# A planner's order for four token blocks: traced durations, layer chains first and steps placed by readiness from the second block on, and a last block without GpSimd

## The chip, the cores and the metric

One core of a Trainium2 chip (trn2) runs the whole program. The metric is the device time of one execution in microseconds (us); several executions of a kernel are timed and their median is compared.

## What is computed

The reference is a causal attention followed by two feed-forward layers, cut here to what matters:

```python
# q, k, v: 4 x 8 heads x 576 x 64;  s: 4 x 8 x 576
scores = q @ k.T / sqrt(64)
cum    = cumsum(max(s, 0))
scores = where(causal, -1e9, scores + min(-(cum_i - cum_j), 0))
attn   = softmax(scores)                    # rows of 576
x      = (attn @ v)                         # 2304 tokens x 512
# layer 1, d_ff 1536
x = ((x @ w_a) * (x @ w_b)) @ w_out
# layer 2, d_ff 2048
h = x @ w_in
g = max(h, 0) + alpha * min(h, 0)
out = g @ w_out
```

All in float32. The kernel keeps that accuracy by cutting each float32 operand into a high and a low part and doing three matmuls for one.

## The kernel before

**Tiling.** The 2304 tokens go through the layers in four blocks of 512, 512, 512 and 768 (`blk` 0 to 3). `ffn` computes one block: layer 1 is a loop over 12 tiles of d_ff (`NF1`), each with two matmul groups in (`into`) and one out, layer 2 a loop over 16 (`NF2`). `mm3` (L1231 to L1233) issues the three matmuls: high by high (`xh`, `wh`), low by high (`xl`), high by low (`wl`); the outs of layer 2 are L1824 to L1826. The last block (`SEVEN` = 3) goes through `ffn_seven` instead, which replaces eight products of half tiles by seven; its tiles `mt`, `th`, `tl` are sums of halves of x, `sw`, `wm`, `wa` sums of weights, `d` partial products.

**What stands between the matmuls.** An intermediate tile is cut on ScalarE (high part: L281) and VectorE or GpSimd (low part: `sub`, L295). The same is done for each weight tile (`wh`, `wl` from `raw`). Weights of the first block, and a third of the second block's, arrive as 64-bit values (`raw<-in_w_dram`) and are decoded by ScalarE (`top`, L1012) and VectorE, and the decoded ones are kept in DRAM (`w_d`) for later blocks.

**Attention as steps.** The attention of the next block is cut into steps (`s01`, `s23`, `s4` for scores and softmax, matmuls at L520; `two_av` for the product with v, matmuls at L845 and L784), and the steps are put between the matmuls of the current block's feed-forward layers. `z` are scores, `zt` their transposes on the way through DRAM (`zd`), `cb` the bias loaded from `cum_d`, `mn` and `sm` the row statistics.

**What sets the order.** Every engine runs its instructions in the order in which they were recorded. The recorder, `Order`, holds a model of the engines' times: `run.now` is TensorE's time in the model, moved on by `run.pe` for each group of matmuls. Work of the other engines is written as chains (`spawn`); `_first` picks the chain whose next instruction can start first by the model, a tie goes to the smaller `time + slack`; `need` runs chains until a given one is done, `pump` runs what can start before `run.now`. `Either` lets the recorder pick GpSimd or VectorE by their modelled time. Three numbers set the model's cost: `gap` (ns added per matmul), `act` and `dve` (ns per instruction on ScalarE and VectorE): `AS_PLANNED` for blocks 0 to 2, `AS_TRACED` for block 3. Steps are put in at a steady rate:

```python
want = min(len(steps), (i + 1) * len(steps) * FASTER / total)
while done < want:
    f, args = steps[done]
    f(*args)
    done += 1
```

where i counts the pieces of the feed-forward layers issued so far.

Of the kernel before, what the change touches and what calls it, by code (L numbers as in the profile page):

```python
# [9 lines left out]
F32 = mybir.dt.float32  # L10
# [5 lines left out]
AF = mybir.ActivationFunctionType  # L16
# [49 lines left out]
FROM_WEIGHTS, AHEAD, FROM_LEAD, FROM_STEPS, STEPS = 2, 10, 3, 4, 3  # L66


FASTER, BEFORE = 1.06, 6


SEVEN, PLAIN_1, PLAIN_2 = 3, 3, 4
SL_SEVEN, SL_BANK = 2500.0, -2000.0
AS_PLANNED, AS_TRACED = (0.0, 90.0, 70.0), (13.3, 170.0, 155.0)
A11, A12, S1, S3, S2, S4, A22 = range(7)


# [29 lines left out]
class Order:  # L107
# [7 lines left out]
    def __init__(self):  # L115
        self.now, self.t, self.n = 0.0, 0.0, 0
        self.free, self.open, self.late = {}, [], LATE
        self.use(AS_PLANNED)

    def use(self, times):  # L120
        self.gap, self.act, self.dve = times

    def spawn(self, gen, ready=None, slack=0.0):
        c = Chain(gen)
# [84 lines left out]
def attention_two_moe_kernel(  # L209
# [77 lines left out]
    def dve(n, rate, f, *args, port=False, **k):  # L287
        yield {"dve2" if port else "dve": run.dve + rate * n}, SEEN
        f(*args, **k)  # L289

    def sub(o, i0, i1, sbuf=True):
        n = size(o)
        t = run.dve + 1.04 * n
        eng = yield Either(pool=115 + 2.17 * n, dve2=t) if sbuf else {"dve": t}, SEEN
        (nc.gpsimd if eng == "pool" else nc.vector).tensor_tensor(o, i0, i1, op=ALU.subtract)  # L295

    def tt(o, i0, i1, op):
        n = size(o)
        eng = yield Either(pool=115 + 2.17 * n, dve2=run.dve + 1.04 * n), SEEN
        (nc.gpsimd if eng == "pool" else nc.vector).tensor_tensor(o, i0, i1, op=op)  # L300

    def scale(o, i, s0, s1):
        n = size(o)
        eng = yield Either(pool=115 + 1.09 * n, dve2=run.dve + 0.52 * n), SEEN
# [21 lines left out]

    ident = const.tile([P, P], F32, name="ident")
    make_identity(nc, ident)
    alpha_sb = small.tile([P, NF2], F32, name="alpha_sb", bufs=1)

    banks = [ps.tile([P, 512], F32, name=f"bank{i}") for i in range(8)]
# [889 lines left out]
    def take():  # L1221
        nonlocal taken
        taken += 1
        prefetch()
        got, ready = loaded[taken - 1]
        run.need(ready)
        return got


# [4 lines left out]
        run.pe(3 * (o.shape[-1] / 2.4 + run.gap))  # L1234

    o_done = {}

    t_hl, pools = [], {}
    H2 = blocks[-1][1] // 2
# [2 lines left out]
    def open_seven():  # L1242

        inner.close()
        big = ctx.enter_context(tc.tile_pool(name="big", bufs=1))

        def big_tile(shape, dtype, tag, bufs=1):
            return big.tile(shape, dtype, name=tag, tag=tag, bufs=bufs)

        pools["big"] = big_tile  # L1250
        t_hl[:] = [
            [big_tile([P, 2, H2], F32R, f"t{j}{i}") for j in "hl"] for i in range(4)
        ]
# [128 lines left out]
    def ffn_seven(blk, sums):  # L1382
# [83 lines left out]

        def rectified_parts(f, got, g, m):
            yield from act(m, g, AF.Relu, scale=-1.0)
            yield from scale(m, m, alpha_sb[:, f:f + 1], -1.0)
            yield from dve(  # L1470
                T, 1.04, nc.vector.scalar_tensor_tensor, g, g, 0.0, m, op0=ALU.max,
                op1=ALU.add, port=True,
            )
            yield from split_g(got, g)
            run.give(of_d, run.t)
# [244 lines left out]
    def ffn(blk):  # L1720
# [5 lines left out]
        def into(j):  # L1726
            wh, wl = take()
            if j in used:
                run.need(used[j])
# [14 lines left out]
        def split_g(f, g):  # L1744
            gh = gp.tile([P, T], F32R, name="gh", tag="gh")
            gl = gp.tile([P, T], F32R, name="gl", tag="gl")
            g_done[f] = gh, gl, run.spawn(split_t(g, gh, gl), run.t)

        def copy_a():
            yield of_t  # L1750
# [37 lines left out]
        for f in range(NF1 + 1):  # L1788
            if f < NF1:
                yield from into(0)  # L1790
                used[0] = run.spawn(copy_a())
                yield from into(1)
                run.need(used[0])
                used[1] = run.spawn(gate(f))
            if f >= 1:
                wh, wl = take()
                gh, gl, ready = g_done.pop(f - 1)
                run.need(ready)
                for d in range(KD):
                    c = slice(d * P, (d + 1) * P)  # L1800
                    o = acc[d][:, 0:T]
                    if f == 1 and d in o_done:
                        run.need(o_done[d])
                    mm3(o, wh[:, c], wl[:, c], gh, gl, f == 1, f == NF1)
                    if f == NF1:
                        x2[d] = run.spawn(
                            split_by(o, xhb[:, d, 0:T], xlb[:, d, 0:T], SHRUNK ** 2)
                        )
                    if d == KD - 1:
                        run.give(of_w)  # L1810
                    yield

        for f in range(NF2 + 2):
            if f < NF2:
                yield from into(f % 2)
                used[f % 2] = run.spawn(rectify(f, ab[f % 2][:, 0:T]))
            if f >= 2:
                wh, wl = take()
                gh, gl, ready = g_done.pop(f - 2)
                run.need(ready)  # L1820
# [23 lines left out]
    for blk in range(NB):  # L1844
        scarce = blk == 0
        run.late = LATE_0 if scarce else LATE
        run.use(AS_TRACED if blk == SEVEN else AS_PLANNED)
        T = blocks[blk][1]
        while x_done[blk]:
            run.need(x_done[blk].pop(0))  # L1850
        steps = plan[blk][1]
        if blk + 1 < NB:
            steps[-BEFORE:-BEFORE] = plan[blk + 1][0]
        if 1 <= blk < NB - 1:
            n = max(0, blk * S + QA - blocks[blk + 1][0])
# [3 lines left out]
        done = 0  # L1859
        if blk == SEVEN:  # L1860
            open_seven()
        for i, _ in enumerate(ffn_seven(blk, sum_x()) if blk == SEVEN else ffn(blk)):
            want = min(len(steps), (i + 1) * len(steps) * FASTER / total)
            while done < want:
                f, args = steps[done]
                f(*args)
                done += 1
        assert done == len(steps)
    while run.open:
        run._run(run._first())  # L1870

# [58 lines left out]
```

## Time and profile before

| | |
|---|---|
| median of 3 executions | 998.69 us (998.48 to 1001.89) |
| the profiled execution: its time, its span in the profile | 998.6 us, 996.6 us |
| PE (TensorE matmuls) busy | 969.5 us, 97% of the span |
| DVE (VectorE) busy | 755.4 us, 76% |
| ACT (ScalarE) busy | 543.4 us, 55% |
| POOL (GpSimd) busy | 310.3 us, 31% |
| first FFN matmuls of blocks 1, 2, 3 | 276.6, 496.7, 717.0 us |

The span is the part of an execution that the profiler shows; 2.0 us lie outside it. Busy time is a sum over the instructions of an engine, so an engine at 97% has 27 us without work in the whole span, and it is there that an order can win or lose time. Times below are from the start of the span.

### The profile page before, as it was taken

To read this page: it belongs to the slowest core of one execution; us is meant where nothing else is said; L and a number is where in the kernel's file an instruction comes from. 1 tells how busy PE (TensorE), PEld (TensorE's weight loads), DVE (VectorE), ACT (ScalarE), POOL (GpSimd) and SP (SyncE) were. 2 spreads that over 40 slices of the span, in tenths; PEclk is the share of its full clock that TensorE was granted. 3 is DMA by queue.
4 is the path that set the end of the run, shared out by engine and by line. 5 is a ranking of instruction groups with operands and counts; after the bars stand their busy time and mean duration, and the time that the engine had idled before them with its cause. 6 is when DMAs were issued, how large, how long until landed. Compare 5 with 4: busy or idle time off the path is not lost.

```text
span 996.6 us, 16041 instructions
## 1 busy us (share of the span) xinstructions
PE 969.5 (97%) x5291; PEld 811.7 (81%) x5291; DVE 755.4 (76%) x1689; ACT 543.4 (55%) x1144; POOL 310.3 (31%) x361
## 2 busy tenths in 40 slices
PE   6999999999999989999999999999999999999998
PEld 4567777778888867888888888888889999988886
DVE  7787777886769667887579877676596888697782
ACT  5966665776656455754555555544452333554342
POOL 2131121431225323442134334231233334252320
PEclk9999999999999999999999999999999999999999
DMA  7699999899688879778498787647312213021101
GB/s 192 189 287 325 340 304 325 300 332 316 233 286 249 270 220 297 227 228 255 142 273 268 220 251 238 207 138 204 141 41 87 65 64 102 26 75 53 63 1 63
DMA packets 140082, 196.77 MB, mean 197 GB/s; under 512 B 35744, under 2 KB 79776, under 8 KB 140000
## 3 DMA queue, kind: packets, MB, share of 16 engines
q1 hardware_dynamic: 130208, 177.93, 57.0%
q10 hardware_dynamic: 9792, 17.83, 4.8%
q8 instruction: 41, 0.67, 0.3%
q14 instruction: 41, 0.34, 0.1%
HBM read 152.13 MB, written 43.59 MB: 196 GB/s over the span
## 4 chain that ended last, share of the span: by engine, by line
PE 85%; DVE 6%; DMA 4%; issue 2%; ACT 2%; SPq 0%; POOL 0%; ACTq 0%; POOLq 0%; DVEq 0%
PE bank L1231 19%; PE bank L1232 18%; PE bank L1233 18%; PE bank L1824 5%; PE bank L1826 4%; PE bank L1825 4%; PE bank L784 3%; DMA raw<-in_w_dram 2%; PE bank L1674 2%; PE bank L1672 2%; PE bank L1673 2%; PE bank L520 2%; PE bank L724 1%; PE bank L546 1%; PE bank L845 1%
## 5 line engine op out<-in xcount | busy, mean ns | idle before, releaser
L1231 PE MATMUL bank<-xh,wh 128*128 128x512 f32 (+1 forms) x620 | 239.9, 387 | 4.5 <-DVE d L289 2.0
L1232 PE MATMUL bank<-xl,wh 128*128 128x512 f32 (+1 forms) x620 | 234.9, 379 | 2.0 <-DVE xl L289 2.0
L1233 PE MATMUL bank<-xh,wl 128*128 128x512 f32 (+1 forms) x620 | 234.6, 378 | 0.0
L281 ACT ACTIVATE wh<-raw 128x512 fp32r<-128x512 f32 (+1 forms) x197 | 114.5, 591 | 84.1 <-PE bank L1232 28.4
L295 POOL TENSOR_TENSOR wl<-raw,wh 128x512 fp32r<-128x512 f32 (+1 forms) x74 | 98.7, 1337 | 161.9 <-ACT wh L281 129.9
L1231 PEld LDWEIGHTS bank<-xh,wh 128*128 128x128 f32 x620 | 116.9, 189 | 30.9 <-issue 5.7
L1232 PEld LDWEIGHTS bank<-xl,wh 128*128 128x128 f32 x620 | 117.0, 189 | 21.8 <-DVE xl L289 3.1
L1233 PEld LDWEIGHTS bank<-xh,wl 128*128 128x128 f32 x620 | 116.7, 188 | 19.0
L273 ACT ACTIVATE z<-z,mn 128x128 f32<-128x128 f32 (+4 forms) x144 | 82.8, 577 | 54.6 <-DVE mn L289 52.8
L295 DVE TENSOR_TENSOR wl<-raw,wh 128x512 fp32r<-128x512 f32 (+1 forms) x130 | 89.4, 694 | 29.4 <-ACT wh L281 26.0
L1231 PE MATMUL bank<-gh,wh 128*128 128x512 f32 (+1 forms) x240 | 89.1, 371 | 0.0
L1233 PE MATMUL bank<-gh,wl 128*128 128x512 f32 (+1 forms) x240 | 88.8, 370 | 0.0
L1232 PE MATMUL bank<-gl,wh 128*128 128x512 f32 (+1 forms) x240 | 88.7, 369 | 0.1
L1012 ACT ACTIVATE top<-raw 128x512 f16<-128x512 bf16 x90 | 69.3, 784 | 27.4 <-DMA raw<-in_w_dram 26.7
L281 ACT ACTIVATE gh<-g 128x512 fp32r<-128x512 f32 x84 | 52.7, 628 | 50.3 <-DVE g L289 48.9
L1824 PE MATMUL bank<-wh,gh 128*128 128x512 f32 x192 | 76.0, 396 | 0.0
L1826 PE MATMUL bank<-wh,gl 128*128 128x512 f32 x192 | 74.8, 390 | 0.0
L1825 PE MATMUL bank<-wl,gh 128*128 128x512 f32 x192 | 74.8, 390 | 0.0
L295 POOL TENSOR_TENSOR wl<-w,wh 128x512 fp32r<-128x512 f32 x31 | 41.2, 1330 | 102.7 <-ACT wh L281 64.3
L295 DVE TENSOR_TENSOR gl<-g,gh 128x512 fp32r<-128x512 f32 x71 | 53.2, 749 | 22.5 <-ACT gh L281 21.3
L599 POOL TENSOR_SCALAR_AFFINE_SELECT z<-z 64x64 f32<-64x64 f32 (+2 forms) x80 | 31.9, 405 | 100.4 <-DVE z L589 74.6
L289 DVE TENSOR_TENSOR d<-bank,mt 128x384 f32<-128x384 f32 x60 | 32.5, 552 | 35.4 <-PE bank L1233 35.4
(157 smaller groups left out, 2033.1 us busy)
## 6 DMA issues: line engine op xcount, KB each, us to landing
raw<-w_d SPq DMA_DIRECT2D x91, 512.0 KB, 4.4
raw<-in_w_dram SPq DMA_DIRECT2D x90, 512.0 KB, 5.6
w_d<-w ACTq DMA_DIRECT2D x46, 256.0 KB, 5.5
zd<-zt SPq DMA_DIRECT2D x48, 192.0 KB, 4.2
pt<-zd SPq DMA_DIRECT2D x48, 192.0 KB, 3.9
kq<-in_kq_a_dram SPq DMA_DIRECT2D x16, 512.0 KB, 6.1
vb<-in_v_dram SPq DMA_DIRECT2D x112, 64.0 KB, 4.5
zd<-zt SPq DMA_DIRECT2D x24, 256.0 KB, 2.8
```

The lines of the kernel that those rows point to most:

```text
L273: nc.scalar.activation(o, i, func, **k)
L281: nc.scalar.activation(o, i, AF.Copy, scale=by)
L289: f(*args, **k)
L295: (nc.gpsimd if eng == "pool" else nc.vector).tensor_tensor(o, i0, i1, op=ALU.subtract)
L599: nc.gpsimd.affine_select(d, d, pattern=pattern, base=0, channel_multiplier=1, compare_op=ALU.is_ge, fill=MASKED,)
L1012: nc.scalar.activation(top.bitcast(F16).rearrange("p (n t) -> p n t", t=2)[:, :, 1], r.bitcast(BF16)[:, 4:4 + 4 * WN].rearrange("p (n t) - ...
L1231: nc.tensor.matmul(o, wh, ih, start=first, stop=False)
L1232: nc.tensor.matmul(o, wh, il, start=False, stop=False)
L1233: nc.tensor.matmul(o, wl, ih, start=False, stop=last)
L1824: nc.tensor.matmul(acc[t], gh[:, c], wh, start=first, stop=False)
L1825: nc.tensor.matmul(acc[t], gh[:, c], wl, start=False, stop=False)
L1826: nc.tensor.matmul(acc[t], gl[:, c], wh, start=False, stop=last)
```

## The change

From block 1 on the recorder uses `AS_TRACED`, which gets a fourth number: a slack of -4000 given to the chains of the feed-forward layers, so that of two instructions that could start at the same time the layer's goes first. Steps are no longer put in at a fixed place: a step that is wanted but whose inputs are not yet there in the model (`possible`) is put off, by up to four steps (`BEHIND`), and where the feed-forward layers would have to wait in the model, a possible step is put in ahead of its time (`wait`), up to four early (`EARLY`). In block 3 `either` offers VectorE alone; there `rectified_parts` makes g with two Relus on ScalarE and one VectorE instruction, in place of one Relu, one `scale` and one VectorE instruction. Block 0 keeps its order.

```diff
-AS_PLANNED, AS_TRACED = (0.0, 90.0, 70.0), (13.3, 170.0, 155.0)
+AS_PLANNED, AS_TRACED = (0.0, 90.0, 70.0, 0.0), (13.3, 170.0, 155.0, -4000.0)
...
+    def either(pool, dve2):
+        return {"dve2": dve2} if run.no_pool else Either(pool=pool, dve2=dve2)
...
-        eng = yield Either(pool=115 + 2.17 * n, dve2=t) if sbuf else {"dve": t}, SEEN
+        eng = yield either(115 + 2.17 * n, dve2=t) if sbuf else {"dve": t}, SEEN
...
+    def seen(*chains):
+        return all(c.done and c.time <= run.now + 100 for c in chains)
+
+    def possible(f, args):
+        rings = 1 if f == two_av else 2
+        if f not in (s01, s23, s4, two_av):
+            return True
+        if not seen(*(reader[i] for i in ring[:rings] if i in reader)):
+            return False
+        if f == two_av:
+            a, b, hp, _ = args
+            keys = [(a, 2 * hp + j, r) for j in range(2) for r in (0, 2, 3)] + [(b, hp, 4)]
+            return all(k in e_t and seen(e_t[k]) for k in keys) and seen(
+                v_t[a, hp, 0][1], v_t[b, hp, 1][1]
+            )
+        b, hp = args[:2]
+        if f == s4:
+            return seen(kq_t[b, hp, 1][1], z_t[b, hp, 4][1])
+        r = args[2] if f == s23 else 0
+        return seen(kq_t[b, hp, 0][1], *(z_t[b, 2 * hp + j, r][1] for j in range(2)))
+
+    def step():
+        f, args = todo.pop(0)
+        f(*args)
+
+    def due():
+
+        while todo and want - (steps_in - len(todo)) > 0:
+            run.pump()
+            if not scarce and want - (steps_in - len(todo)) < BEHIND and not possible(*todo[0]):
+                return
+            step()
+
+    def wait(*chains):
+
+        run.pump()
+        while not scarce and not seen(*chains) and todo and possible(*todo[0]):
+            if steps_in - len(todo) - want >= EARLY:
+                break
+            step()
+            run.pump()
+        run.need(*chains)
...
             yield from act(m, g, AF.Relu, scale=-1.0)
-            yield from scale(m, m, alpha_sb[:, f:f + 1], -1.0)
+            yield from act(g, g, AF.Relu)
             yield from dve(
-                T, 1.04, nc.vector.scalar_tensor_tensor, g, g, 0.0, m, op0=ALU.max,
-                op1=ALU.add, port=True,
+                T, 1.04, nc.vector.scalar_tensor_tensor, g, m, less_alpha[:, f:f + 1], g,
+                op0=ALU.mult, op1=ALU.add, port=True,
             )
...
             for k in range(KD):
                 if k in x2:
-                    run.need(x2[k])
+                    wait(x2[k])
...
-                used[1] = run.spawn(gate(f))
+                used[1] = run.spawn(gate(f), slack=run.ffn)
...
-        run.use(AS_TRACED if blk == SEVEN else AS_PLANNED)
+        run.use(AS_TRACED if blk else AS_PLANNED)
+        run.no_pool = blk == SEVEN
```

All other waits of `take`, `into` and `ffn` become `wait` in the same way, and `copy_a`, `rectify`, `split_t` and the split between the layers get the same slack.

**What that does to the order.** TensorE has the same 4765 matmuls. In block 1 a few attention steps stand 3 to 12 matmuls elsewhere; in block 2 the third `two_av` stands ahead of the last out group of layer 1 (12 matmuls) rather than behind it; in block 3 nothing moves. VectorE's instructions go from 1691 to 1733, ScalarE's from 1070 to 1089 (16 of them are the second Relu), GpSimd's from 363 to 303. In block 3 GpSimd's go from 77 to none. Of these, 76 stand on VectorE now: 60 of 128x256 (`wm` 26, `sw` 24, `wa` 5, `wl` 5), 10 of 128x768 (`gl` 6, `tl` 3, `mt` 1) and 6 of 128x512 (`wl`); 15 scalings of 128x768 that VectorE had are gone. In blocks 1 and 2 GpSimd has 17 instructions more.

**Place 1, the third `s4` step of block 1.** VectorE before (`z,mn<-bank,z` is the add of the bias with the row statistic, which frees the bank for the next matmul of the step):

```order
L295 TENSOR_TENSOR qs<-kq,qs 64x512
L305 TENSOR_SCALAR z<-z,sm 128x512
L589 TENSOR_SCALAR z<-cb_3818,cumq 128x256
L289 STREAM_TRANSPOSE zt<-z 128x512
L589 TENSOR_SCALAR z<-cb_4013,cumq 128x256
L289 ISA z,mn<-bank_98,z 128x288
L289 ISA mn 128x1
L295 TENSOR_TENSOR wl<-raw,wh 128x512
L289 ISA z,mn<-bank_99,z 128x288
L289 ISA mn 128x1
L295 TENSOR_TENSOR wl<-raw,wh 128x512
```

And the same place after, with bank numbers one higher:

```order
L290 STREAM_TRANSPOSE zt<-z 128x512
L290 RECIPROCAL sm<-sm 128x1
L309 TENSOR_SCALAR z<-z,sm 128x512
L594 TENSOR_SCALAR z<-cb_3815,cumq 128x256
L290 STREAM_TRANSPOSE zt<-z 128x512
L290 ISA z,mn<-bank_99,z 128x288
L290 ISA mn 128x1
L290 ISA z,mn<-bank_100,z 128x288
L290 ISA mn 128x1
L290 TENSOR_TENSOR mn<-mn 128x1
L299 TENSOR_TENSOR wl<-raw,wh 128x512
```

The low part of a weight (`wl`) no longer stands between the two adds, and one of the two biases (`z<-cb`) ahead of them has gone elsewhere.

**Place 2, the end of layer 1 in block 1.** TensorE before (`xh_107` and `xl_109` are the block's x, rewritten in four quarters as input of layer 2):

```order
L1231 MATMUL bank_105<-gh,wh 128x512
L1232 MATMUL bank_105<-gl,wh 128x512
L1233 MATMUL bank_105<-gh,wl 128x512
L1231 MATMUL bank_100<-xh_107,wh 128x512
L1232 MATMUL bank_100<-xl_109,wh 128x512
L1233 MATMUL bank_100<-xh_107,wl 128x512
L1231 MATMUL bank_100<-xh_107,wh 128x512
L1232 MATMUL bank_100<-xl_109,wh 128x512
```

TensorE after:

```order
L1236 MATMUL bank_106<-gh,wh 128x512
L1237 MATMUL bank_106<-gl,wh 128x512
L1238 MATMUL bank_106<-gh,wl 128x512
L1236 MATMUL bank_101<-xh_108,wh 128x512
L1237 MATMUL bank_101<-xl_110,wh 128x512
L1238 MATMUL bank_101<-xh_108,wl 128x512
L850 MATMUL bank_99<-pb,vb 64x64 x10
L789 MATMUL bank_100<-pt_115,vb 64x128
```

A `two_av` step now follows the first three matmuls of layer 2; before it came twelve matmuls later. ScalarE at the same place before:

```order
L281 ACTIVATE wh<-raw 128x512
L281 ACTIVATE xh_107<-bank_102 128x512
L281 ACTIVATE xh_107<-bank_103 128x512
L281 ACTIVATE xh_107<-bank_104 128x512
L1012 ACTIVATE top_136<-raw 128x512
L281 ACTIVATE xh_107<-bank_105 128x512
```

And after:

```order
L282 ACTIVATE wh<-raw 128x512
L282 ACTIVATE xh_108<-bank_103 128x512
L1017 ACTIVATE top_137<-raw 128x512
L282 ACTIVATE xh_108<-bank_104 128x512
L282 ACTIVATE xh_108<-bank_105 128x512
L282 ACTIVATE xh_108<-bank_106 128x512
```

The decode of a weight (`top`) stands behind the first quarter of x now, before it stood behind the third.

**Place 3, the start of block 3.** GpSimd before, from the last instructions of block 2 on:

```order
L295 TENSOR_TENSOR wl<-raw,wh 128x512 x4
L300 TENSOR_TENSOR mt<-mt 128x768
L300 TENSOR_TENSOR sw<-raw 128x256
L295 TENSOR_TENSOR tl_8159<-mt,th_8158 128x768
L295 TENSOR_TENSOR tl_8163<-mt,th_8162 128x768
L295 TENSOR_TENSOR tl_8165<-mt,th_8164 128x768
L295 TENSOR_TENSOR wm<-sw,wm 128x256 x2
```

VectorE after, where these now stand among its own (`d<-bank,d` is the gate's product, for which a bank waits):

```order
L290 TENSOR_TENSOR d<-bank_102,d 128x384
L304 TENSOR_TENSOR mt<-mt 128x768
L304 TENSOR_TENSOR mt<-xh_107,mt 128x768
L304 TENSOR_TENSOR mt<-mt,xl_109 128x768
L290 TENSOR_TENSOR d<-bank_102,d 128x384
L304 TENSOR_TENSOR mt<-mt,xh_108 128x768
L304 TENSOR_TENSOR mt<-xh_108,mt 128x768
L299 TENSOR_TENSOR tl_8162<-mt,th_8161 128x768
L304 TENSOR_TENSOR mt<-mt,xl_110 128x768
L290 TENSOR_TENSOR d<-bank_102,d 128x384
L299 TENSOR_TENSOR tl_8160<-mt,th_8159 128x768
```

The `mt` and the `tl` that GpSimd had (`tl_8159`, now `tl_8160`) are on VectorE, between the `d` products.

## Rows read from the trace of the kernel before

**Rows 1.** Busy time by stage (windows): each engine, granted PE clock, DMA share, GB/s.

```profile
276.60:496.70 220.10, 214.91 (x1138) 177.31 (x1137) 164.14 (x385) 121.93 (x257) 76.01 (x94) 0.99 0.77 242
496.70:717.00 220.30, 220.21 (x1234) 181.87 (x1233) 163.53 (x400) 116.63 (x251) 72.35 (x96) 1.00 0.71 218
717.00:996.60 279.60, 271.79 (x1447) 249.49 (x1445) 213.03 (x345) 116.50 (x241) 91.42 (x77) 1.00 0.19 60
743.40:846.40 103.00, 102.70 (x582) 96.58 (x581) 81.66 (x144) 35.55 (x84) 36.62 (x34) 1.00 0.27 84
372.00:375.20 3.20, 3.20 (x9) 2.48 (x8) 2.80 (x9) 1.92 (x5) 1.50 (x1) 0.54 0.88 268
```

**Rows 2.** Waits of TensorE, 276.6 to 997: total us, times, longest.

```profile
PE bank L1231 <- DVE d L289: 2.3, 2, 2.0
PE bank L520 <- DVE ovl L295: 2.0, 1, 2.0
PE bank L1232 <- DVE xl L289: 1.8, 2, 1.6
PE bank L1231 <- DVE mt L289: 1.7, 1, 1.7
PE bank L520 <- DVE mn L289: 1.4, 2, 0.7
```

**Rows 3.** Timeline of TensorE at the end of layer 1, block 1.

```profile
395.22 0.50 PE L1232 MATMUL bank<-xl,wh 128*128 128x512 f32 x1 [1.60 <-DVE xl L289]
395.55 0.39 PE L1233 MATMUL bank<-xh,wl 128*128 128x512 f32 x1
```

**Rows 4.** Timeline of ScalarE in block 1, near 352 (start, duration, instruction).

```profile
351.84 0.79 ACT L1012 ACTIVATE top<-raw 128x512 f16<-128x512 bf16 x1 [2.02 <-DMA raw<-in_w_dram]
```

**Rows 5.** Timeline of VectorE at the third s4 step of block 1.

```profile
369.13 0.79 DVE L295 TENSOR_TENSOR wl<-raw,wh 128x512 fp32r<-128x512 f32 x1
```

**Rows 6.** Timeline of VectorE ahead of the wait at 395.22.

```profile
392.68 0.52 DVE L589 TENSOR_SCALAR z<-cb,cumq 128x576 f32<-128x576 f32 x1 [2.39 <-DMA cb<-cum_d]
```

**Rows 7.** Timeline of ScalarE at the end of layer 1, block 1.

```profile
395.79 0.80 ACT L1012 ACTIVATE top<-raw 128x512 f16<-128x512 bf16 x1 [2.44 <-DMA raw<-in_w_dram]
```

**Rows 8.** Timeline of SP, which issued the load of cb.

```profile
384.75 0.80 SPq L311 DMA_DIRECT2D zd<-zt  x2
...
386.09 0.86 SPq L311 DMA_DIRECT2D cb<-cum_d  x1
```

**Rows 9.** The chain that ended last, 340 to 360: a two_av step.

```profile
345.55 0.73 PE bank L845 x20
346.28 2.19 PE bank L784 x40
```

**Rows 10.** Timeline of VectorE at the start of block 3.

```profile
727.79 2.60 DVE L295 TENSOR_TENSOR tl<-mt,th 128x768 fp32r<-128x768 f32 x1
732.85 2.60 DVE L295 TENSOR_TENSOR gl<-d,gh 128x768 fp32r<-128x768 f32 x1
735.38 2.04 DVE L295 TENSOR_TENSOR wl<-raw,wh 128x256 fp32r<-128x256 f32 x1
```

**Rows 11.** VectorE's groups by form, 717 to 997 (busy us, mean ns, idle before).

```profile
L289 DVE TENSOR_TENSOR d<-bank,mt 128x384 f32<-128x384 f32 x60 | 32.5, 552 | 35.4 <-PE bank L1233 35.4
...
L295 DVE TENSOR_TENSOR gl<-d,gh 128x768 fp32r<-128x768 f32 x22 | 23.3, 1060 | 0.4
L295 DVE TENSOR_TENSOR wm<-sw,wm 128x256 fp32r<-128x256 f32 x34 | 21.3, 651 | 0.4 <-ACT wm L281 0.4
L295 DVE TENSOR_TENSOR wl<-raw,wh 128x512 fp32r<-128x512 f32 x27 | 20.8, 785 | 2.7 <-ACT wh L281 2.5
...
L305 DVE TENSOR_SCALAR mt<-mt,alpha_sb 128x768 f32<-128x768 f32 x12 | 9.0, 776 | 0.0
L300 DVE TENSOR_TENSOR sw<-sw,raw 128x256 f32<-128x256 f32 x14 | 5.8, 416 | 0.0
```

**Rows 12.** Timeline of GpSimd at the start of block 3.

```profile
732.22 4.92 POOL L295 TENSOR_TENSOR tl<-mt,th 128x768 fp32r<-128x768 f32 x2 [2.64 <-ACT th L281]
```

More of the change, by code (lines that the diff above doesn't have):

```diff
@@ L66 @@
 FROM_WEIGHTS, AHEAD, FROM_LEAD, FROM_STEPS, STEPS = 2, 10, 3, 4, 3
-FASTER, BEFORE = 1.06, 6
+FASTER, BEFORE, BEHIND, EARLY = 1.06, 6, 4, 4
 SEVEN, PLAIN_1, PLAIN_2 = 3, 3, 4
 SL_SEVEN, SL_BANK = 2500.0, -2000.0
-AS_PLANNED, AS_TRACED = (0.0, 90.0, 70.0), (13.3, 170.0, 155.0)
+AS_PLANNED, AS_TRACED = (0.0, 90.0, 70.0, 0.0), (13.3, 170.0, 155.0, -4000.0)
 A11, A12, S1, S3, S2, S4, A22 = range(7)
@@ L118, in __init__ @@
         self.use(AS_PLANNED)
+        self.no_pool = False
     def use(self, times):
-        self.gap, self.act, self.dve = times
+        self.gap, self.act, self.dve, self.ffn = times
     def spawn(self, gen, ready=None, slack=0.0):
@@ L298, in tt @@
         n = size(o)
-        eng = yield Either(pool=115 + 2.17 * n, dve2=run.dve + 1.04 * n), SEEN
+        eng = yield either(115 + 2.17 * n, dve2=run.dve + 1.04 * n), SEEN
         (nc.gpsimd if eng == "pool" else nc.vector).tensor_tensor(o, i0, i1, op=op)
@@ L303, in scale @@
         n = size(o)
-        eng = yield Either(pool=115 + 1.09 * n, dve2=run.dve + 0.52 * n), SEEN
+        eng = yield either(115 + 1.09 * n, dve2=run.dve + 0.52 * n), SEEN
         (nc.gpsimd if eng == "pool" else nc.vector).tensor_scalar(
@@ L328, in attention_two_moe_kernel @@
     make_identity(nc, ident)
+    less_alpha = small.tile([P, NF2], F32, name="less_alpha", bufs=1)
     alpha_sb = small.tile([P, NF2], F32, name="alpha_sb", bufs=1)
@@ L1225, in take @@
         got, ready = loaded[taken - 1]
-        run.need(ready)
+        wait(ready)
         return got
@@ L1236, in attention_two_moe_kernel @@
     o_done = {}
+    todo, want = [], 0
+    def seen(*chains):
[34 more added lines that the diff above has]
+        run.need(*chains)
     t_hl, pools = [], {}
@@ L1250, in open_seven @@
         pools["big"] = big_tile
+        nc.vector.tensor_scalar(less_alpha, alpha_sb, -1.0, None, op0=ALU.mult)
         t_hl[:] = [
@@ L1728, in into @@
             if j in used:
-                run.need(used[j])
+                wait(used[j])
             for k in range(KD):
                 if k in x2:
-                    run.need(x2[k])
+                    wait(x2[k])
                 c = slice(k * P, (k + 1) * P)
@@ L1746, in split_g @@
             gl = gp.tile([P, T], F32R, name="gl", tag="gl")
-            g_done[f] = gh, gl, run.spawn(split_t(g, gh, gl), run.t)
+            g_done[f] = gh, gl, run.spawn(split_t(g, gh, gl), run.t, run.ffn)
         def copy_a():
@@ L1790, in ffn @@
                 yield from into(0)
-                used[0] = run.spawn(copy_a())
+                used[0] = run.spawn(copy_a(), slack=run.ffn)
                 yield from into(1)
-                run.need(used[0])
-                used[1] = run.spawn(gate(f))
+                wait(used[0])
+                used[1] = run.spawn(gate(f), slack=run.ffn)
             if f >= 1:
@@ L1797, in ffn @@
                 gh, gl, ready = g_done.pop(f - 1)
-                run.need(ready)
+                wait(ready)
                 for d in range(KD):
@@ L1806, in ffn @@
                         x2[d] = run.spawn(
-                            split_by(o, xhb[:, d, 0:T], xlb[:, d, 0:T], SHRUNK ** 2)
+                            split_by(o, xhb[:, d, 0:T], xlb[:, d, 0:T], SHRUNK ** 2), slack=run.ffn
                         )
@@ L1815, in ffn @@
                 yield from into(f % 2)
-                used[f % 2] = run.spawn(rectify(f, ab[f % 2][:, 0:T]))
+                used[f % 2] = run.spawn(rectify(f, ab[f % 2][:, 0:T]), slack=run.ffn)
             if f >= 2:
@@ L1819, in ffn @@
                 gh, gl, ready = g_done.pop(f - 2)
-                run.need(ready)
+                wait(ready)
                 first, last = f == 2, f == NF2 + 1
@@ L1858, in attention_two_moe_kernel @@
         total = NF1 * 3 * KD + NF2 * (KD + T // P)
-        done = 0
+        todo[:], steps_in, want = steps, len(steps), 0
         if blk == SEVEN:
@@ L1862, in attention_two_moe_kernel @@
         for i, _ in enumerate(ffn_seven(blk, sum_x()) if blk == SEVEN else ffn(blk)):
[L1863 to L1868, printed above, removed]
+            want = min(steps_in, (i + 1) * steps_in * FASTER / total)
+            due()
+        while todo:
+            step()
     while run.open:
```

## The prediction

> **What bounds the kernel now.** I read the busy time by stage first. In block 2 (496.7 to 717.0) TensorE is busy 220.21 of 220.30 us: there the matmuls alone set the time, and no order of the other engines can make it shorter. In block 1 it is busy 214.91 of 220.10, in block 3 271.79 of 279.60 [rows 1]. The changed kernel has the same matmuls, so a gain can only come out of those gaps, and a loss needs a new one. VectorE is the next engine: 164.14 of 220.10 in block 1, 213.03 of 279.60 in block 3.
>
> Then the waits of TensorE from block 1 on. There are five rows with eight waits, 9.2 us in all, and every one is released by VectorE [rows 2]. Three of the rows are in block 1 (`ovl`, `xl`, `mn`), two in block 3 (`d`, `mt`). A wait also costs a little behind itself: the matmul after the one at 395.22 takes 0.50 us and the next 0.39 [rows 3]; I put that at 0.1 us a wait. So all waits of the five rows are worth 9.2 + 8 x 0.1 = 10.0 us. One more loss is no wait: from 372.00 to 375.20 TensorE works without a gap at a granted clock of 0.54, so mostly at 1.2 GHz in place of 2.4 [rows 1]. That costs 3.2 x (1 - 0.54) = 1.5 us. What the engine did before is the `s4` step with two of the eight waits, so I count the two together; that the fall goes with the waits is my choice. The best that the order could give is thus 10.0 + 1.5 = 11.5 us.
>
> Last the timelines at each wait, to see what VectorE itself was late for; there lies the answer to what the new order can do.
>
> **The change, part by part.** The sum is made against the profiled execution, 998.6 us, which is the median (998.69) less 0.1.
>
> *Block 1, the wait for `ovl` (2.0 us).* The chain behind it begins on ScalarE: a decode (`top`) stood 2.02 us for its raw weight [rows 4], and the cut of x stood behind it. What is late is a DMA, and these instructions stand in the same order after the change. Gain 0; bounds 0 and 2.1.
>
> *Block 1, the third `s4` step (two waits, 1.4 us).* Each matmul of the step waits until VectorE has read the bank before it. Between the two reads stood a low part of a weight, 0.79 us [rows 5], and ahead of the first stood two biases, one of which is gone there (place 1). Each wait is at most 0.7 [rows 2], so taking away 0.79 ends the second, and one bias less (0.52 for a `z<-cb` of 576 columns [rows 6]) most of the first. Gain 1.4 + 0.2 = 1.6, and the clock's 1.5 with it; bounds 0 and 3.1.
>
> *Block 1, the end of layer 1 (two waits, 1.8 us).* Two loads are late here. VectorE stood 2.39 us for a bias, `cb` [rows 6], with the low parts of x behind it: the wait of 1.60 [rows 3]. ScalarE stood 2.44 us for a raw weight [rows 7], with the fourth quarter of x behind it: the other 0.2. SP had issued that `cb` at 386.09, behind two stores (0.80 us for both) [rows 8]; in the new order one of the two stands behind the load, so it lands some 0.4 to 0.6 us earlier, and the first wait shrinks to about 1.0. The decode now stands ahead of three quarters of x rather than one, which alone would make things worse by up to two waits. But a `two_av` step follows the first three matmuls, and such a step takes 0.73 + 2.19 = 2.92 us [rows 9], more than the 2.44 for which ScalarE stood. If that cover were gone, the 2.44 would be paid. Gain 1.8 + 0.2 - 1.0 = 1.0; bounds -1.5 and 2.0.
>
> *Block 2.* The third `two_av` goes from behind the last out group of layer 1 to ahead of it. Behind that group it covered the cut of x for layer 2 with 2.92 us; now nothing does. In block 1 the same uncovered place cost 1.6, with a load late as well; without the load I take 0.5. Bounds 0 and 1.7.
>
> *Block 3 (three waits, 4.0 us; 4.3 with the 0.1 behind each).* The gate's product `d` waited behind `gl` (2.60 us) and `wl` (2.04 us) on VectorE [rows 10]. A `gl` takes 1.06 on average and a quarter-size difference 0.416 [rows 11], so these two alone were late by 1.5 and 1.6. At the same time GpSimd ran `tl`, 732.22 to 737.14 [rows 12]; `wl` ends at 737.42, right behind it. VectorE's instruction with two inputs stands until GpSimd's ends. Without GpSimd that goes, but its work comes to VectorE: two to three `tl` of 1.06 in that stretch against the 3.1 us of stretching given back. So I count 4.0 of the 4.3, and leave 0.3 for the moved `tl`, which stand between the `d` products (place 3). Bounds 0 and 4.3. The second Relu in layer 2 is ScalarE's, which is busy 116.50 of 279.60 [rows 1], and the scaling that it replaces (0.776 us, fifteen of them) leaves VectorE: cost nothing, by that cover.
>
> The Trainium skill, "SBUF — State Buffer", section "SBUF: two separate sides", has the port pair that VectorE and GpSimd share as a lock held for a whole instruction, with the other blocked. By that rule, which the end of `wl` agrees with, the 17 instructions more that GpSimd gets in blocks 1 and 2 would each hold VectorE up there, and the outcome would be rival two's.
>
> *A wait that I can't name.* Two blocks are ordered anew, with 440 us in which hundreds of instructions change places, against a block 2 without a single wait now. I count one new wait of the middle size of the longer ones seen (0.7, 0.7, 1.6, 1.7, 2.0, 2.0), 1.5. Bounds 0 and three such.
>
> *Sum:* -1.6 - 1.5 - 1.0 - 4.0 + 0.5 + 1.5 = -6.1 on 998.6: **992.5 us**. It lies between 989.2 (all but the `ovl` wait won and nothing new: 11.5 less 2.1 is 9.4) and 995.0 (the end of layer 1 and the clock not won).
>
> **The rivals.**
>
> *One: in block 1 nothing moves.* At two of its three places a late load stands up the chain: ScalarE or VectorE stood 2.02, 2.39 and 2.44 us for DMAs [rows 4, 6, 7], at a DMA share of 0.77 in the block [rows 1]. The order doesn't make them land earlier, and if the `s4` step's two biases only change places with something as long, its waits and the clock's fall come again. For it: the new recorder has no late loads in mind, and a decode stands further ahead in ScalarE's order than before. Against it: place 1 waited for no load. Then 998.6 - 4.0 + 0.5 + 1.5 = 996.6. Chance 0.22.
>
> *Two: layer chains first makes attention late.* With the new slack a layer's chain wins every tie, and the bank reads of the steps (`z,mn`) stand behind it. A late step costs 1.6 (the two waits at place 1), and a fall of the clock 1.5. With block 3's gain and nothing of block 1's, four such steps and one more fall give 998.6 - 4.0 + 4 x 1.6 + 1.5 = 1002.5; two of them and no fall 997.8. I put it at 1000.5. For it: GpSimd has 17 instructions more in these blocks, and one beside it made `gl` 1.5 us longer. Against it: VectorE is busy only 75% there, and steps are put off in the model until their inputs are there. Chance 0.14.
>
> *Three, on the other side: VectorE becomes the bound of block 3.* In nine product units of layer 1 (743.4 to 846.4) VectorE is busy 81.66 of 103.00 us, and GpSimd has 34 instructions [rows 1]. Moved at 0.416 each [rows 11] they make VectorE 95.8 us, 93%; at 0.651, the mean of the `wm` that VectorE runs beside GpSimd, 103.8, which is over. It decides from (103.00 - 81.66)/34 = 0.63 us each. At GpSimd's own 36.62/34 = 1.08 VectorE would need 118.3, 15.3 too much; I take the middle of 0.8 and 15.3, 8 us. With block 3's gain lost and the rest kept: 998.6 - 1.6 - 1.5 - 1.0 + 0.5 + 1.5 + 8 = 1004.5. Over the whole block, with the larger ones at 1.06 (10) and 0.785 (6) and the fifteen scalings off, VectorE comes to 213.03 + 60 x 0.416 + 10.6 + 4.7 - 11.6 = 241.7, 86%. For it: at 93% in order, a bank read is easily late. Against it: 0.651 is a time beside GpSimd, which won't be there. Chance 0.10. The Trainium skill, "Perfetto Trace Analysis", section "Identifying the Most-Contended Engine", takes the busy share of VectorE as a fair measure of how near it is to its limit; by it this move goes to the wrong engine, and the outcome would be this rival's.
>
> **How the numbers follow.** The forecast has 0.54, with a range of its own of 989.2 to 995.0. The range reaches to rival two's figure and, with some room for waits that no row names, past the forecast's lower end: 988 to 1001. It leaves out rival three (most of 0.10), the upper part of rival two (0.05) and some 0.03 below. A measurement here tells about 0.5% from no change, 5.0 us: faster is below 993.7, slower above 1003.7. Faster: three quarters of the forecast and little of rival one, 0.44. Slower: 0.06 of rival three and 0.04 of rival two, 0.10. Same: the rest, 0.46.
>
> **What would show it.** In the changed profile: the stretched VectorE instructions at the start of block 3 back at about 1 us, and no wait for `d` over 0.5; no wait for `mn` in block 1 and no stretch below a clock of 0.9 after it; the waits for `ovl` (2) and `xl` (1) still there; at most one or two new rows of waits in blocks 1 and 2. VectorE's busy time from 717 on near 242 us, with `wm` at about 0.42. Wrong would be the sum if bank reads in block 3 wait in most units, or if block 2 shows waits for `mn` or `xl` of several us.

## The result, and the profile after

The changed kernel takes 991.83 us (median of 6, 989.19 to 994.74), the kernel before on the same chip 1000.27 us (median of 6, 998.48 to 1003.52): a ratio of 0.9916, 95% interval 0.9894 to 0.9937. That is 8.4 us less. The forecast was 6.1 less, 992.5, with a range of 988 to 1001.

The profiled execution took 994.1 us, 992.0 of them in the span. Where the time went is read from the start of the first feed-forward matmul of each block and of the last matmul of all (worked out from the starts of the matmuls in the trace):

| | before | after | difference |
|---|---|---|---|
| up to block 1's first (TensorE's order the same in both) | 276.56 | 279.93 | +3.4 |
| block 1 | 220.11 | 219.32 | -0.8 |
| block 2 | 220.29 | 220.00 | -0.3 |
| block 3, to the last matmul | 275.58 | 268.69 | -6.9 |
| from there to the end of the span | 4.1 | 4.1 | 0 |

So this execution lost 3.4 us ahead of block 1, where next to nothing was changed (two low parts of weights, for one, stand on VectorE that were GpSimd's), and gained 8.0 behind it. Its time alone would show little more than half of that gain. The stages show it.

The busy time by stage, as in [rows 1] (time, then busy us of PE, PEld, DVE, ACT and POOL, granted clock, DMA share, GB/s):

```profile
279.93:499.25 219.32, 215.43 (x1137) 178.23 (x1136) 166.90 (x380) 123.69 (x257) 83.82 (x99) 0.98 0.77 243
499.25:719.25 220.00, 220.00 (x1234) 181.74 (x1232) 156.10 (x385) 118.44 (x254) 83.22 (x110) 1.00 0.72 219
719.25:992.00 272.75, 269.08 (x1447) 250.17 (x1445) 207.60 (x405) 128.82 (x257) 0.00 (x0) 1.00 0.18 62
```

In block 3 TensorE now runs without a gap up to its last matmul: from 719.25 to 987.94 it is busy for all of the 268.69 us. VectorE has 60 instructions more there (405 for 345) and is busy for *less* time, 207.60 us for 213.03. The groups by form (operation, tiles and shape) say why; these answer to [rows 11] (busy us, mean ns):

```profile
L290 DVE TENSOR_TENSOR d<-bank,mt 128x384 f32<-128x384 f32 x60 | 33.3, 555 | 24.3 <-PE bank L1238 23.9
L299 DVE TENSOR_TENSOR gl<-d,gh 128x768 fp32r<-128x768 f32 x28 | 26.7, 953 | 3.2 <-ACT gh L282 3.0
...
L299 DVE TENSOR_TENSOR wm<-sw,wm 128x256 fp32r<-128x256 f32 x60 | 24.9, 418 | 0.0
L299 DVE TENSOR_TENSOR wl<-raw,wh 128x512 fp32r<-128x512 f32 x33 | 22.2, 686 | 4.5 <-ACT wh L282 4.4
```

A `wm` takes 0.418 us where it took 0.651, so 60 of them cost 24.9 us and the 34 before cost 21.3. `d<-bank,mt`, with one input in a bank, is as long as before. The start of block 3 in the timeline of VectorE, against [rows 10]:

```profile
730.07 0.95 DVE L299 TENSOR_TENSOR tl<-mt,th 128x768 fp32r<-128x768 f32 x1
...
732.50 0.95 DVE L299 TENSOR_TENSOR tl<-mt,th 128x768 fp32r<-128x768 f32 x1
...
734.90 0.95 DVE L299 TENSOR_TENSOR gl<-d,gh 128x768 fp32r<-128x768 f32 x1
735.77 0.42 DVE L299 TENSOR_TENSOR wl<-raw,wh 128x256 fp32r<-128x256 f32 x1
736.18 0.56 DVE L290 TENSOR_TENSOR d<-bank,d 128x384 f32<-128x384 f32 x1
```

What took 2.60, 2.60 and 2.04 us (`tl`, `gl`, `wl`) takes 0.95, 0.95 and 0.42, in the rows at 730.07, 734.90 and 735.77. The `tl` at 732.50 is one that GpSimd had. It stands between VectorE's own now, and `d` comes on time all the same.

TensorE's waits from block 1 to the end, against [rows 2]:

```profile
PE bank L525 <- DVE ovl L299: 3.6, 1, 3.6
PE bank L525 <- DVE xl L299: 0.3, 1, 0.3
```

The waits for `d`, `mt`, `mn` and for `xl` at the end of layer 1 are gone. The one for `ovl` has grown, and the row for `xl` of 0.3 is new. Here are, for `ovl`, the instruction of ScalarE that stands for a load, as in [rows 4], the matmul that waits, and the stretch behind it in the windows:

```profile
357.43 0.77 ACT L1017 ACTIVATE top<-raw 128x512 f16<-128x512 bf16 x1 [2.48 <-DMA raw<-in_w_dram]
```

```profile
360.14 0.79 PE L525 MATMUL bank<-kh,qs 128*128 128x512 f32 x1 [3.58 <-DVE ovl L299]
```

```profile
360.00:366.00 6.00, 5.86 (x14) 4.60 (x15) 3.38 (x8) 3.52 (x7) 1.32 (x1) 0.50 0.78 261
```

For 6 us behind the wait the granted clock is 0.50, that is 1.2 GHz, and 6.00 x (1 - 0.50) = 3.0 us are lost. So most of what block 1 won at its other places it gave back here: this wait and the clock's fall behind it cost 6.6 us together. Before, the wait for `ovl` was 2.0, and the clock's fall, at another place, cost 1.5.

### The profile page after: what moved, and what is told of

Same layout as the page of the kernel before. It is cut to its first block, busy times and chain, and to the rows that moved or that the text cites. A ratio compares the mean times of both kernels' runs of the same rounds, so it can differ in the third digit from the quotient of the medians.

```text
span 992.0 us, 15984 instructions
## 1 busy us (share of the span) xinstructions
PE 970.8 (98%) x5291; PEld 816.2 (82%) x5291; DVE 747.0 (75%) x1731; ACT 560.0 (56%) x1163; POOL 233.7 (24%) x301
## 4 chain that ended last, share of the span: by engine, by line
PE 82%; DMA 8%; DVE 5%; issue 2%; ACT 2%; POOL 0%; SPq 0%; ACTq 0%; DVEq 0%; POOLq 0%
PE bank L1236 18%; PE bank L1237 18%; PE bank L1238 18%; PE bank L1874 5%; PE bank L1876 4%; PE bank L1875 4%; DMA raw<-in_w_dram 3%; PE bank L1723 2%; PE bank L1722 2%; PE bank L1724 2%; PE bank L789 2%; PE bank L525 2%; DMA cb<-cum_d 2%; DMA zd<-zt 1%; PE bank L729 1%
## 5 line engine op out<-in xcount | busy, mean ns | idle before, releaser
L299 POOL TENSOR_TENSOR wl<-raw,wh 128x512 fp32r<-128x512 f32 x72 | 97.0, 1349 | 130.9 <-ACT wh L282 76.6
L299 DVE TENSOR_TENSOR wl<-raw,wh 128x512 fp32r<-128x512 f32 (+1 forms) x132 | 82.1, 635 | 33.9 <-ACT wh L282 28.7
L1017 ACT ACTIVATE top<-raw 128x512 f16<-128x512 bf16 x90 | 69.5, 785 | 24.9 <-DMA raw<-in_w_dram 23.2
L299 DVE TENSOR_TENSOR gl<-g,gh 128x512 fp32r<-128x512 f32 x74 | 56.8, 767 | 20.3 <-ACT gh L282 19.6
L299 POOL TENSOR_TENSOR wl<-w,wh 128x512 fp32r<-128x512 f32 x29 | 38.6, 1330 | 101.1 <-ACT wh L282 54.2
L290 DVE STREAM_TRANSPOSE zt<-z 128x384 f32<-128x384 f32 (+2 forms) x88 | 56.6, 651 | 2.2 <-POOL z L585 1.0
L282 ACT ACTIVATE wh<-w 128x512 fp32r<-128x512 f32 x67 | 41.6, 626 | 21.7 <-DVE w L290 7.4
```

Source lines behind the costliest of these rows:

```text
L282: nc.scalar.activation(o, i, AF.Copy, scale=by)
L1017: nc.scalar.activation(top.bitcast(F16).rearrange("p (n t) -> p n t", t=2)[:, :, 1], r.bitcast(BF16)[:, 4:4 + 4 * WN].rearrange("p (n t) - ...
```

## The experiments

All times are medians; each ratio is to the kernel before on the same chip, whose medians were 1002.02, 1002.61 and 1001.60 us in the three sets.

**The two halves.** First block 3 alone: the kernel before, with this line and the `either`, `less_alpha` and two Relus of the change:

```diff
...
+        run.no_pool = blk == SEVEN
...
```

> Blocks 0 to 2 as before; block 3 as in the change (no GpSimd, two Relus). Theory: the gain of the change sits in block 3, where GpSimd made VectorE's two-input instructions longer. In the two traces block 3 went from 275.6 to 268.7 us, so this kernel should be 5 to 7 us faster than before, near 994, with no wait of TensorE after 720 and the block 1 waits (ovl 2.0, mn 1.4, xl 1.8) as before. Rival: the order of blocks 1 and 2 gives most of it, and block 3's difference is in part its other start; then at most 3 us, 997 or more.

Measured: 992.06 us, ratio 0.9907 (0.9877 to 0.9936). Block 3 takes 268.69 us, the very figure of the change, and from its start to the end of the span VectorE is busy 208.61 of 272.80. Blocks 1 and 2 take 220.8 and 220.3. The ratio is that of the change within its interval, so the theory stands: the larger part sits in block 3. What was expected of block 1's waits is a miss, though. These are all of TensorE's from block 1 on:

```profile
PE bank L525 <- DVE ovl L299: 3.3, 1, 3.3
PE bank L1237 <- DVE xl L290: 1.6, 1, 1.6
PE bank L525 <- DVE xl L299: 0.7, 1, 0.7
```

VectorE, ScalarE and GpSimd have block 1 in the very order of the kernel before, and yet the waits for `mn` are not there, `ovl` is 3.3 rather than 2.0, and the clock falls behind `ovl`, ahead of the third `s4` step. At that step a `wl` of 0.78 us still stands between the two adds, at 375.46. So the waits of block 1 move from one execution to the next with one and the same order.

Then the other half, the change without this line and with `rectified_parts` as before:

```diff
-        run.no_pool = blk == SEVEN
```

> The other half: blocks 1 and 2 ordered as in the change, block 3 with GpSimd and one Relu as before. Theory: 1 to 3 us faster than before, near 998, and TensorE's waits for d and mt in block 3 back, some 4 us. Rival: blocks 1 and 2 carry the change; then 4 us or more, 996 or less.

Measured: 998.77 us, ratio 0.9962 (0.9938 to 0.9987), 3.3 us faster. Block 1 takes 217.7 us, block 2 219.9. Block 3 takes 277.9, and its waits are back, as the waits of TensorE say:

```profile
PE bank L1236 <- DVE d L290: 2.6, 3, 1.8
...
PE bank L1236 <- DVE mt L290: 1.7, 1, 1.7
```

Here the clock falls behind two of these waits, from 737.1 and from 894.1 (0.66 in the 5 us from 736 and from 893), which it did not in the kernel before. By 5 x (1 - 0.66) each that is some 3.4 us, more than the 2.3 by which this block 3 is longer than before.

The halves add up to 13 us, more than the whole measured alone (8.4) or beside others (11.6, below); the intervals are some 3 us to either side.

**Is it GpSimd's running, or its results coming late?** Both go when its work is moved. This kernel is the change, which keeps the moved work on VectorE, and it lets GpSimd run on a tile of its own:

```diff
+        idle = big_tile([P, 512], F32, "idle")
+        nc.gpsimd.memset(idle, 0.0)
+        for _ in range(140):
+            nc.gpsimd.tensor_tensor(idle, idle, idle, op=ALU.subtract)
```

> The change, and in block 3 also 140 GpSimd subtractions of 128x512 on a tile of their own, which no other engine reads or waits for (extra work, not part of the computation). If what made block 3 slow was GpSimd working beside VectorE, VectorE's instructions with two SBUF inputs get longer again (0.42 to 0.65 and more for wm, 0.95 to over 1.5 for gl) and TensorE waits for d and mt: 4 to 15 us slower than the change, 996 to 1007. Rival: it was the path through GpSimd, its results coming late, not its mere running; then the time is the change's, 992, and wm stays at 0.42.

Measured: 1058.74 us, ratio 1.0579 (1.0543 to 1.0615), some 67 us more than the change, where 4 to 15 were expected. Block 3 takes 336.1 us. Nothing waits for these instructions, so their running alone does it. The control has the same with memsets:

```diff
-            nc.gpsimd.tensor_tensor(idle, idle, idle, op=ALU.subtract)
+            nc.gpsimd.memset(idle, 0.0)
```

> The change, and in block 3 also 140 GpSimd memsets of 128x512 on a tile that nobody else reads (extra work, not part of the computation): the control of e3_port, GpSimd just as often at work, but reading nothing from SBUF. Theory: VectorE's instructions with two inputs stand only beside a GpSimd instruction that reads SBUF; then wm stays at 0.42, block 3 at 268.7 us and the time at the change's 992. Rival: any work of GpSimd does it; then wm is 0.6 or more, and the time some tens of us longer, as with e3_port (1058.7).

Measured: 989.47 us, ratio 0.9891 (0.9858 to 0.9924), the change's time; block 3 takes 268.69 us. A memset takes 0.53 us and a subtraction 1.3 on average, so the two can be set side by side only while both run: the first 70 us of block 3. Windows (as in the table of stages) and groups there, with subtractions:

```profile
714.60:784.60 70.00, 51.14 (x249) 47.04 (x248) 67.17 (x61) 20.40 (x43) 66.00 (x52) 0.88 0.13 44
```

```profile
L299 DVE TENSOR_TENSOR wm<-sw,wm 128x256 fp32r<-128x256 f32 x8 | 9.4, 1198 | 0.0
```

And with memsets:

```profile
714.30:784.30 70.00, 70.00 (x402) 67.59 (x402) 56.59 (x110) 30.59 (x67) 63.17 (x119) 1.00 0.20 67
```

```profile
L299 DVE TENSOR_TENSOR wm<-sw,wm 128x256 fp32r<-128x256 f32 x17 | 6.9, 417 | 0.0
```

GpSimd is as busy in both, 66.00 and 63.17 of 70 us. Beside instructions that read SBUF a `wm` takes 1.198 us, VectorE gets through 61 instructions rather than 110, and TensorE does 249 matmuls rather than 402, with the clock falling too (0.88). Beside instructions that only write, a `wm` takes 0.417 and nothing is lost. The timelines of VectorE and GpSimd with subtractions show how:

```profile
728.25 1.79 DVE L304 TENSOR_TENSOR mt<-xh,mt 128x768 f32<-128x768 f32 x1
729.97 1.79 DVE L299 TENSOR_TENSOR tl<-mt,th 128x768 fp32r<-128x768 f32 x1
```

```profile
719.03 11.92 POOL L1304 TENSOR_TENSOR idle<-idle 128x512 f32<-128x512 f32 x7
```

Each engine is at 1.7 to 1.8 us an instruction (11.92/7 = 1.70 for GpSimd), where VectorE's take 0.95 when alone; the next `d<-bank,d` keeps its 0.54. The Trainium skill, "SBUF — State Buffer", section "SBUF: two separate sides", says just this: a VectorE instruction with two SBUF inputs and a GpSimd instruction that reads SBUF exclude each other for a whole instruction. The trace agrees as to who stands for whom, down to the memsets and to `d`, which has one input in a bank. Of the whole instruction it shows most but not all: from 777 to 781, where every VectorE instruction has an input in a bank, a subtraction takes 1.04 us, and 0.95 + 1.04 = 1.99 in a row is more than the 1.70 measured, so the two run side by side for some 0.3 us.

**Does the second Relu count?** The change with the scaling on VectorE again:

```diff
-            yield from act(g, g, AF.Relu)
+            yield from scale(m, m, alpha_sb[:, f:f + 1], -1.0)
...
```

> The change without the second Relu: the scaling of 128x768 by alpha stands on VectorE again, without GpSimd in block 3. Theory: it is the taking away of GpSimd that counts, and the Relu adds nothing that can be seen: block 3 within 1 us of 268.7, the time 992. Rival: VectorE needed the room (the scalings are some 9 to 12 us of its work there); then waits for d or mt come back and block 3 takes 271 us or more.

Measured: 992.44 us, ratio 0.9902 (0.9867 to 0.9937). Block 3 takes 268.69 us again, with VectorE busy 213.25 of 272.80. The second Relu is worth nothing here; taking GpSimd away is all of block 3's gain.

**The three parts of the new order in blocks 1 and 2, one taken away at a time.** Without the slack:

```diff
-AS_PLANNED, AS_TRACED = (0.0, 90.0, 70.0, 0.0), (13.3, 170.0, 155.0, -4000.0)
+AS_PLANNED, AS_TRACED = (0.0, 90.0, 70.0, 0.0), (13.3, 170.0, 155.0, 0.0)
```

> The change with the slack of the layers' chains at 0 (layer chains no longer first). Theory: in blocks 1 and 2 the slack is one of three small parts; the time within 2 us of the change, 990 to 994, with one or two waits for the layers' tiles (gh, gl, xl) back in block 1 or 2. Rival: the slack makes all of the gain there, and without it blocks 1 and 2 are back at 220.1 and 220.3 us, 994 to 996.

Measured: 992.44 us, ratio 0.9909 (0.9876 to 0.9941). A wait for `g` of 1.1 us is new, block 1 takes 221.2, block 2 219.95. The wait for `ovl` is 4.1 us here, the longest of all runs, with the clock at 0.50 for the 6 us from 355 on, so block 1's figure doesn't tell what the slack is worth. Without the readiness rule:

```diff
-FASTER, BEFORE, BEHIND, EARLY = 1.06, 6, 4, 4
+FASTER, BEFORE, BEHIND, EARLY = 1.06, 6, 0, -9999
```

> The change with steps put in at the fixed places again (none put off, none early). Theory: the readiness rule covers the wait at the end of layer 1 (a two_av step pulled ahead); without it the waits for xl are back there, 1.8 us or more, as before, and the time is 993 to 996. Rival: the place of the steps does nothing and the time is the change's, 992.

Measured: 994.76 us, ratio 0.9932 (0.9906 to 0.9958). Block 1 takes 220.2, block 2 221.8, with two waits in it (`z` 0.7, `gl` 0.6). At the end of layer 1 of block 1 stand these:

```profile
PE bank L1237 <- DVE xl L290: 1.0, 2, 0.8
PE bank L1236 <- ACT xh L282: 0.6, 1, 0.6
```

The 0.8 is the wait for the first quarter of x, behind a late `cb`, which the change has too when it is run again (0.8, below). The 0.6 for `xh` and the other 0.2 for `xl` stand behind a decode that waited 2.45 us for its load. The change has nothing there, as its `two_av` stands at that place: in the repeat a decode waited 2.39 us without any wait of TensorE behind it. Without the traced durations, in the last set, with the change itself run again beside it:

```diff
-        run.use(AS_TRACED if blk else AS_PLANNED)
+        run.use(AS_TRACED if blk == SEVEN else (0.0, 90.0, 70.0, -4000.0) if blk else AS_PLANNED)
```

> The change with the old, shorter modelled durations in blocks 1 and 2 (slack and readiness kept). Theory: traced durations matter as little as the slack; within 2 us of the change run beside it, block 3 at 268.7. Rival: the shorter durations make the model think everything is there, so that readiness and slack do nothing right: blocks 1 and 2 back at 220 us each or above, 994 to 997.

> The change itself again, on the same chip as the two others. Theory and rival agree: 0.988 to 0.994 of before; it is here so that e8_planned, e9_lands9 and the change can be set side by side.

Measured: 995.84 us, ratio 0.9932 (0.9909 to 0.9955), and for the change 990.05, ratio 0.9878 (0.9857 to 0.9899). The theory fails here: the traced durations are worth more than the 2 us allowed, and the rival's figures are met. The waits of TensorE without them:

```profile
PE bank L525 <- DVE ovl L299: 4.4, 2, 3.3
PE bank L1237 <- DVE xl L290: 2.8, 1, 2.8
```

Block 1 takes 223.1 us and block 2 220.2, against 217.4 and 219.9 for the change beside it. By the medians it costs 5.8 us to go without the durations, and the two intervals don't meet. What the slack and the readiness rule are worth by themselves the runs leave open: 0.9909 and 0.9932 against 0.9916 and 0.9878 for the change in two sets.

**The wait that the change doesn't mend.** If the decode stands for its load ahead of the cuts of x, a model in which raw weights land later should put it behind them:

```diff
-LATE, LATE_0 = 1000.0, 1300.0
+LATE, LATE_0, LANDS = 1000.0, 1300.0, 6000.0
...
-            yield from dma(r.bitcast(U16)[:, 1:1 + 4 * WN], w64[i].bitcast(U16))
+            yield {"sp": 480}, 700
+            nc.sync.dma_start(r.bitcast(U16)[:, 1:1 + 4 * WN], w64[i].bitcast(U16))
+            yield {"dma": 4 * WN * P / 180}, 900 + (LANDS if n >= NW else 0.0)
```

> The change, with the model's time for a raw weight's landing in block 1 made 6.0 us longer, so that the recorder puts the decode (top) behind the cuts of x for which it stood ahead in the change. Theory: the wait for ovl (3.6 us in the change) and the fall of the clock behind it (6 us at half speed, about 2.8 us lost) come from the decode standing for its load on ScalarE ahead of these cuts; without it block 1 is 3 to 6 us shorter than the change, 986 to 989. Rival: the load is late for the layer itself, and the wait only moves to the weight (wh) that is decoded from it: 990 to 994.

Measured: 989.47 us, ratio 0.9874 (0.9847 to 0.9901). The wait for `ovl` is gone and the granted clock is 1.00 in every 5 us of block 1; block 1 takes 216.1 us. A wait for `xl` of 1.6 is there, and two for weights are new (`wl` 0.6, `wh` 0.2), so a little of the rival's came too. As its interval overlaps the change's, it was run again beside the change, and with a larger number:

> e4_lands6 again beside the change. Theory: the decode that stood for its load costs the change the wait for ovl and the clock's fall behind it, in most executions: 2 to 5 us less than the change run beside it, and no wait for ovl. Rival: the 2.4 us between their medians were another chip's state; then both agree within 1 us.

> The change with a raw weight's landing in block 1 modelled 9.0 us longer, where e4_lands6 had 6.0. Theory: 6.0 already took the decodes away from ahead of x; more brings nothing, or lets the weight itself come late for the layer (waits for wh or wl): 988 to 992. Rival: loads still stand ScalarE up at the end of layer 1, and 9.0 removes the waits for xl of 1.8 us too: 986 to 988.

Measured: with 6.0 us 990.81, ratio 0.9890 (0.9858 to 0.9922); with 9.0 us 989.17, ratio 0.9861 (0.9837 to 0.9885); the change 990.05. The block agrees with the theory: 215.7 and 215.1 us for the change's 217.4. With 6.0 a wait for `xl` of 1.5 is there again and one for `wl` of 0.6; all waits of TensorE from block 1 on with 9.0 are these:

```profile
PE bank L1240 <- POOL wl L299: 0.6, 1, 0.6
PE bank L1238 <- ACT wh L282: 0.6, 1, 0.6
```

The change beside it has these:

```profile
PE bank L525 <- DVE ovl L299: 2.3, 1, 2.3
PE bank L1237 <- DVE xl L290: 0.8, 1, 0.8
```

The time of the whole program doesn't show it: the intervals overlap, and with 6.0 the median is not below the change's at all. So the cause of the `ovl` wait is shown: in the change ScalarE's decodes stand six times in block 1 for their loads, 9.8 us in all, in the three executions where the load is modelled to land later not once, and in all three the wait is gone. (Their order differs from the change's in other places of the block too.) That this makes a faster kernel isn't shown.

## Why the prediction was right, step by step

**Block 3, -4.0: right in its mechanism, too small.** It gained 6.9 us. The three waits hold 4.6 of it, from start to start. The other 2.3 are in small delays, which the list of waits doesn't give. Set side by side, matmul by matmul, 94 starts follow 0.01 to 0.35 us later before than in the change (2.1 us in all) and 35 as much earlier (0.4); the rest is smaller still. "All waits of the five rows are worth 10.0" was therefore no upper bound for the order's gain, and the term was 2.9 too small. That GpSimd's reading of SBUF stretches VectorE is shown by e3_port against e3_memset.

**VectorE's busy time in block 3, 242: wrong.** It is 207.6. The sum of rival three added the moved work, most of it at the undisturbed 0.416 us, to 213.0 us of work at disturbed prices. But nearly all the two-input work there was stretched, not only the rows at the start and `wm`: `wl` of 512 went from 0.785 to 0.686, `gl` from 1.06 to 0.95. So rival three was never near. Its test, 0.63 us for each moved instruction, is passed by 0.42.

**The third `s4` step, -1.6: the waits went, but that the new order took them away isn't shown.** All six executions with the change's order in block 1 have no wait at this step. Nor has e1_block3, with the old order there: the wait for `ovl` had grown and the clock had fallen ahead of it, and TensorE came to the step at 377.57, when VectorE had done both reads (the second from 376.17 to 376.62). In e2_blocks12, with the new order, the clock doesn't fall ahead of the step and no wait comes, which speaks for the order; it is one execution.

**The clock, -1.5: failed in the profiled execution.** "I count the two together" was the step. What the runs showed in its place: the fall left the `s4` step and came back behind the wait for `ovl`, at 3.0 us. It is not tied to one wait: with this order in block 1 it came behind `ovl` in the change (wait 3.6 us), e3_port (3.0), e3_memset (3.1), e5_one_relu (3.8) and e10_change (2.3), but not in e2_blocks12 (2.7); with the old order it came behind `ovl` in e1_block3 (3.3), but not before (2.0). With the wait gone (e4_lands6, e9_lands9, e11_lands6) there was no fall in block 1.

**The wait for `ovl`, gain 0: right as to cause.** ScalarE still stands for the load (2.48 us). The size was wrong: the wait moves from one execution to the next, 2.3 to 3.8 us in six with this order in block 1, against 2.0 and 3.3 in two with the old one.

**The end of layer 1, -1.0: right on average, by few executions.** In the profiled execution both waits are gone, a gain of 2.0. But of the six with this order three have no wait here, and the others 0.8 (e10_change), 1.6 (e5_one_relu) and 2.4 us (e2_blocks12): the load of `cb` is still late in some. The mean is 0.8, against 1.8 and 1.6 with the old order. That the `two_av` covers the decode's load is borne out: in e2_blocks12 the decode stood 3.98 us and no wait came behind it, while without the cover, in e7_fixed_steps, 2.45 us cost 0.8.

**Block 2, +0.5, and a wait without a name, +1.5: failed.** Block 2 takes 220.00 us, 0.3 less than before, and the only new row is 0.3 us, in block 1. Nothing came of the +0.5: the third `two_av` was not missed as a cover.

**The sum: nearer than its terms, which is luck in part.** By stage the forecast had -4.1 for block 1, +0.5 for block 2, -4.0 for block 3 and +1.5 for the wait without a name. The profiled execution has -0.8, -0.3 and -6.9. So block 1 won 3.3 less than forecast, block 3 won 2.9 more, and the 2.0 of new costs didn't come: the errors cancel in part. The time also starts from a lucky figure: the forecast counts from 998.6, while the median before is 1000.27 with more executions. The gain was forecast at 6.1 and is 8.4, 2.3 apart, the times are 992.5 and 991.83, 0.7 apart, and below 993.7, the prediction's own mark for faster, to which it gave 0.44. What the prediction had right without luck is where most of the gain lies, block 3, and why.

**The rivals.** One (only block 3 gains) is nearer than I gave it: e1_block3 has the change's time within the intervals, and in the profiled execution block 1 won only 0.8. What speaks against it is e2_blocks12, 3.3 us faster with an interval clear of 1, and block 1 with the new order at 217.0 to 220.2 us in six executions (mean 218.1), against 220.1 and 220.8 in two with the old. Two (attention late) didn't come: in the profiled execution blocks 1 and 2 took no longer than before.

**What stays open.** Why the granted clock falls behind some of these waits and not others, and how much of the change's gain lies in block 1: the stretch ahead of it varies from 276.0 to 281.9 us between executions with nearly the same order there, a spread that is more than the block's whole gain.

## What to carry to other kernels

Price a moved instruction, and those that stay behind, by rows in which the engine that is taken away is idle; a mean over disturbed rows hides the gain. In this kernel GpSimd's work beside VectorE instructions with two SBUF inputs saved VectorE next to nothing: in block 3 of e5_one_relu VectorE has 75 instructions more than before (420 for 345) for 0.2 us more of its time (213.25 for 213.03). When a whole-program time varies by several us ahead of the change, read the stages, and look for late loads on an in-order engine before the order itself. And don't credit an order with a wait that is gone before the old order has been profiled more than once: here it lost the same wait by itself.

## What was not expected

With 140 GpSimd subtractions that nobody waits for, block 3 went from 268.7 to 336.1 us, while the same number of memsets cost nothing. And block 3 without GpSimd's reads takes 268.69 us in all eleven runs that have it so, to the hundredth, where the blocks with attention and DMA traffic vary by some us.
